# Block-sparse attention with a channel mix on one core: another order of the units, one finishing pass, and other numbers in the planner

## The chip, the cores and the metric

The kernel runs on one core of a Trainium2 chip. The core has four compute engines, each with its own instruction stream: TensorE (PE, matrix multiplies, with its weight loads shown as PEld), VectorE (DVE), ScalarE (ACT) and GpSimd (POOL). SyncE (SP) issues the DMA transfers here. The engines run side by side and wait for one another on semaphores. The metric is the device time of one execution in microseconds; less is better.

## The reference

The inputs are q, k and v (batch 4, 8 heads, 768 positions, 64 channels), a table of sampled blocks, two mixing vectors and three weight matrices. Positions are grouped into 24 blocks of 32. A block of queries looks at itself and its two neighbours, at the first and the last block, and at three sampled blocks; the first and the last block look at everything. On the attention's output stands a channel mix:

```python
scores = np.where(mask, scale * np.matmul(q, k.transpose(0, 1, 3, 2)), -1000000000.0)
attn = np.exp(scores - np.max(scores, axis=-1, keepdims=True))
attn = attn / (np.sum(attn, axis=-1, keepdims=True) + 1e-09)
x = np.matmul(attn, v)          # then laid out as (batch, 768, 512)
xk = mu_k * x + (1.0 - mu_k) * x_prev      # x_prev: one position back
xr = mu_r * x + (1.0 - mu_r) * x_prev
k = np.maximum(xk @ w_k, 0.0)              # 512 -> 1024
v = k * k @ w_v                            # 1024 -> 512
out = (1.0 / (1.0 + np.exp(-(xr @ w_r)))) * v
```

## The kernel before

**Units and tiles.** The attention is done in 26 units. A *wide* unit takes the first and the last block of one batch against all keys (4 of them, one for each batch); a *near* unit takes block n of all four batches against its eight blocks (22 of them, n = 1 to 22, called n1 to n22 below). The channel mix is done in 12 tiles of two blocks each: tile t takes blocks 2t and 2t+1 of all batches, and for the position before them the last row of block 2t−1. So tile 1 needs n1, n2 and n3, while tiles 0 and 11 need all four wide units.

**A near unit** loads q (scaled on POOL), keys into the buffer KA and values into VA; it computes scores (`s`, PE) in two halves of four heads, the row maximum (`nm`, DVE), the exponential (`p`, ACT), transposes (`t` on PE, copied to `pt` by ACT or DVE), the product with the values (`o`, PE), the division by the row sum (`R`, `x`, DVE), and a last transpose (`tx`, PE) that ACT copies into the tile `xt`. A wide unit does the same with names that carry a w: `sw`, `nmw`, `pw`, `tw`, `ptw`. KA and VA are one buffer each, which wide and near units share: a wide unit takes half of KA, and near units hold the last three blocks in a ring of slots and the sampled blocks in slots of their own.

**A tile of the mix** is split into a high and a low part (`xr`, `xk`: POOL, DVE, ACT and POOL in turn), then come on PE two gates (`r`, 12 multiplies each), four hidden groups (`h`, 24 each) and two value sums (`v`, 24 each), since every product is made of three.

**Weights.** The 20 pieces of w_r, w_k and w_v arrive as 64-bit numbers of 512 KB each. Each is turned into 32 bits by one ACT pass and three DVE passes (L379, L383, L387) and split into a high and a low part (L397 or L399, and L401). The first twelve go through eight buffers `early_w`.

**The order of the work** is planned: each step is handed to a planner with an engine, a cost in ns, the buffers that it reads and writes, and a due time. The planner places the steps one at a time, by due time among those that can start soon, with its own costs of hops between engines, of transfers and of the matmul clock. Each engine's instruction stream, SP's queue of transfers among them, is the result, and each engine works strictly in that order. The due times are the tables at the end of the file (`UNIT_AT`, `MIX_AT`, `RAW_AT`, `WEIGHT_AT` and the offsets). In this kernel the four wide units come first:

```python
return [[(b, 0), (b, NB - 1)] for b in range(B)] + [[(b, n) for b in range(B)] for n in range(1, NB - 1)]
```

and the tiles of the mix run from 0 to 11. The accumulator of a near unit is two buffers of one bank, `o[0]` and `o[1]`, for four heads each, and `finish` divides each by itself.

## Time and profile before

| | |
|---|---|
| runs | 573.17, 574.13, 574.96 us; median 574.13 |
| the profiled execution | 573.36 us |
| its span, from the first to the last instruction | 571.5 us |
| busy: PE, PEld, DVE, ACT, POOL | 538.0, 441.8, 262.3, 295.2, 317.1 us |
| mean granted TensorE clock | 0.987 of full speed |
| moved by DMA | 86.08 MB, 151 GB/s over the span |
| chain that ended last | PE 75%, DMA 9%, POOL 7%, DVE 4% |

The span is read in stretches: in each, the engine (or the DMA) that is busy nearly all the time sets the pace there. In the order of time one sees a start of some 100 us in which transfers are close to their limit and PE sits idle for parts, and then a long stretch in which PE is busy throughout. The timeline of one engine tells when its groups of instructions began and what ended the idle time in front of them; the chain of waits tells which work ended last.

### The profile page before, as it was taken

To read this page: it belongs to the slowest core of one execution; us is meant where nothing else is said; L and a number is where in the kernel's file an instruction comes from. 1 tells how busy PE (TensorE), PEld (TensorE's weight loads), DVE (VectorE), ACT (ScalarE), POOL (GpSimd) and SP (SyncE) were. 2 spreads that over 40 slices of the span, in tenths; PEclk is the share of its full clock that TensorE was granted. 3 is DMA by queue.
4 is the path that set the end of the run, shared out by engine and by line. 5 is a ranking of instruction groups with operands and counts; after the bars stand their busy time and mean duration, and the time that the engine had idled before them with its cause. 6 is when DMAs were issued, how large, how long until landed. Compare 5 with 4: busy or idle time off the path is not lost.

```text
span 571.5 us, 18262 instructions
## 1 busy us (share of the span) xinstructions
PE 538.0 (94%) x7724; PEld 441.8 (77%) x7724; DVE 262.3 (46%) x481; ACT 295.2 (52%) x594; POOL 317.1 (55%) x377
## 2 busy tenths in 40 slices
PE   8678768999999999999999999999999999999997
PEld 3445545777797897897897887897798898989896
DVE  1677998864434324337325345415434424242401
ACT  2536477675656445467456456556555543424241
POOL 1322657897465384475275456466167265677670
PEclk8979998999999999999999999999999999999999
DMA  8999899734442624454543272445323000000001
GB/s 319 367 387 367 303 315 346 267 120 147 133 148 78 220 77 129 154 169 132 194 142 114 93 225 89 146 160 188 117 89 95 21 21 19 18 21 18 33 5 38
DMA packets 34181, 86.08 MB, mean 151 GB/s; under 512 B 5010, under 2 KB 5780, under 8 KB 31124
## 3 DMA queue, kind: packets, MB, share of 16 engines
q1 hardware_dynamic: 34100, 84.92, 44.2%
q8 instruction: 61, 1.00, 0.7%
q14 instruction: 20, 0.16, 0.1%
HBM read 78.60 MB, written 6.29 MB: 149 GB/s over the span
## 4 chain that ended last, share of the span: by engine, by line
PE 75%; DMA 9%; POOL 7%; DVE 4%; SPq 3%; issue 2%; ACT 1%; POOLq 0%; ACTq 0%
PE v L821 23%; PE o L586 7%; PE s L562 6%; PE t L526 6%; PE r_0p L774 5%; PE h_0p L792 5%; PE r_1p L774 5%; PE h_3p L792 5%; PE h_2p L792 5%; PE h_1p L792 5%; DMA q<-qt 3%; DMA VA<-vw 2%; DMA KA<-kt 2%; POOL q L464 2%; PE tx L666 2%
## 5 line engine op out<-in xcount | busy, mean ns | idle before, releaser
L821 PE MATMUL v<-wv,k 128*128 128x512 f32 (+1 forms) x600 | 144.8, 391 | 1.1 <-POOL wv L401 1.1
L821 PEld LDWEIGHTS v<-wv,k 128*128 128x128 f32 x600 | 106.6, 188 | 24.5 <-POOL wv L401 1.5
L542 ACT ACTIVATE p<-s,nm 128x256 f32<-128x256 f32 x176 | 71.7, 484 | 20.6 <-DVE nm L570 20.5
L464 POOL TENSOR_SCALAR q<-q 128x512 f32<-128x512 f32 (+1 forms) x26 | 36.6, 1409 | 45.8 <-DMA q<-qt 25.1
L570 DVE TENSOR_REDUCE nm<-s 128x4 f32<-128x1024 f32 x44 | 52.8, 1217 | 13.5 <-PE s L562 13.1
L530 ACT COPY pt<-t 128x512 f32<-128x512 f32 x68 | 39.6, 587 | 37.4 <-PE t L526 34.8
L526 PE MATMUL t<-ident,p 128*128 128x128 f32 x352 | 54.5, 278 | 3.8 <-ACT pt L530 2.1
L586 PEld LDWEIGHTS o<-VA,pt 128*32 128x32 f32 x2816 | 42.2, 109 | 13.3 <-issue 10.4
L586 PE MATMUL o<-VA,pt 128*32 128x65 f32 x2816 | 49.5, 222 | 2.9 <-ACT pt L530 1.9
L526 PEld LDWEIGHTS t<-ident,p 128*128 128x128 f32 x352 | 40.6, 141 | 14.8 <-ACT pt L530 2.9
L562 PE MATMUL s<-KA,q 64*32 64x256 f32 x1408 | 44.9, 383 | 4.0 <-DMA KA<-kt 1.7
L750 POOL TENSOR_TENSOR xr<-xr_1f,xr 128x256 fp32r<-128x256 f32 x24 | 17.9, 744 | 38.5 <-ACT xr L748 38.5
L829 DVE SCALAR_TENSOR_TENSOR z<-v,z 128x512 f32<-128x512 f32 (+1 forms) x25 | 16.7, 669 | 48.4 <-PE v L821 48.4
L741 DVE SCALAR_TENSOR_TENSOR xr_1f<-xr_1d,mk,xt 128x128 f32<-128x128 f32 x48 | 17.1, 355 | 47.5 <-POOL xr L750 39.7
L738 POOL TENSOR_TENSOR xr_1d<-xt 128x128 f32<-128x128 f32 x48 | 20.5, 427 | 31.8 <-DVE xr_1f L741 24.0
L792 PE MATMUL h_1p<-xk,wk 128*128 128x256 f32 x288 | 36.9, 282 | 0.0
L562 PEld LDWEIGHTS s<-KA,q 64*32 64x32 f32 x1408 | 25.2, 106 | 15.1 <-issue 2.4
L792 PE MATMUL h_0p<-xk,wk 128*128 128x256 f32 x288 | 36.8, 282 | 0.0
L774 PE MATMUL r_0p<-wr,xr 128*128 128x512 f32 x144 | 36.7, 400 | 0.0
L792 PE MATMUL h_3p<-xk,wk 128*128 128x256 f32 x288 | 36.5, 281 | 0.0
L792 PE MATMUL h_2p<-xk,wk 128*128 128x256 f32 x288 | 36.1, 281 | 0.0
L738 POOL TENSOR_TENSOR xr_0d<-xt 128x128 f32<-128x128 f32 x48 | 19.4, 403 | 30.1 <-DVE xr_0f L741 20.7
(138 smaller groups left out, 962.4 us busy)
## 6 DMA issues: line engine op xcount, KB each, us to landing
VA<-vt SPq DMA_DIRECT2D x93, 260.0 KB, 3.8
KA<-kt SPq DMA_DIRECT2D x90, 256.0 KB, 3.7
VA<-vw SPq DMA_DIRECT2D x24, 260.0 KB, 6.5
KA<-kq SPq DMA_DIRECT2D x16, 384.0 KB, 6.4
out<-z SPq DMA_DIRECT2D x23, 256.0 KB, 2.0
q<-qt SPq DMA_DIRECT2D x22, 256.0 KB, 4.3
early_w<-w_k SPq DMA_DIRECT2D x8, 512.0 KB, 7.3
raw<-w_v SPq DMA_DIRECT2D x8, 512.0 KB, 6.1
```

The lines of the kernel that those rows point to most:

```text
L464: plan.add(POOL, 90 + 0.95 * HP * many * BLK, due, lambda: nc.gpsimd.tensor_scalar(out=q.ap[:, 0 : HP * many * BLK], in0=q.ap[:, 0 : HP * ...
L526: nc.tensor.transpose(tp.ap[:, i, :], p.ap[:, x : x + P], ident.ap)
L530: plan.add(ACT, 200 + 0.75 * P * many, rank + 0.1, lambda: nc.scalar.copy(pt.ap[:, 0:many], tp.ap[:, 0:many]), reads=[(tp,)], writes=[(pt,)])
L542: plan.add(ACT, 262 + 0.83 * width, rank, lambda: nc.scalar.activation(p.ap[:, out], view(), AF.Exp, bias=nm()), reads=[(s,), key[0]], wri ...
L562: nc.tensor.matmul(s.ap[ROWS[j], row, a * 256 : (a + 1) * 256].rearrange("p (c x t) -> p c t x", c=2, t=QB), q.ap[half, (hp * QB + j) * BL ...
L570: nc.vector.tensor_reduce(out=nm.ap.rearrange("p (r a) -> p r a", r=2), in_=s.ap.rearrange("p r (a x) -> p r a x", a=2), axis=AX.X, op=ALU ...
L586: nc.tensor.matmul(o[gi].ap[ROWS[j], i * DV : (i + 1) * DV], pts[row].ap[:, 2 * a + g, ROWS[j]], VA.ap[:, c0 + g, j, h * DV : (h + 1) * DV ...
L738: sub.tensor_tensor(out=parts(d.ap), in0=cols(c, 0), in1=cols(c, 1), op=ALU.subtract)
L750: plan.add(POOL, 80 + 2.4 * MIX * tw, rank + O_MIX, lambda f=f, cs=cs: nc.gpsimd.tensor_tensor(out=dst.ap[:, 1, cs], in0=f.ap, in1=dst.ap[ ...
L774: nc.tensor.matmul(pr.ap[:, 0:512], xr.ap[:, a, c, :], wr.ap[:, w, c, :], start=(c == 0 and m == 0), stop=(c == CC - 1 and m == 2))
L792: nc.tensor.matmul(ph.ap[:, ff * TT : (ff + 1) * TT], wk.ap[:, w, c, f * P : (f + 1) * P], xk.ap[:, a, c, :], start=(c == 0 and m == 0), s ...
L821: nc.tensor.matmul(pv.ap[:, 0:width], k2.ap[:, a, f, i * P : (i + 1) * P], wv.ap[:, w, f, cs], start=(f == 0 and m == 0), stop=(f == FC - ...
```

## The change

The change has four parts. The first two say what is computed when; the third changes the numbers and rules with which the order is planned; the fourth moves some work between engines or buffers.

1. One wide unit comes first, then the 22 near units, then the three other wide units. The tiles run in the order 1 to 10, 0, 11.
2. A near unit's accumulator is one buffer of two banks. `finish` makes one sum pass, one reciprocal and one product over all eight heads, where it made two of each. From unit 5 on the scores of both halves are one step for the planner.
3. The planner counts a slowdown of DVE beside POOL, has other costs (q's scaling on POOL, the weight passes, the mix), counts large transfers at a smaller size, and all due times are new.
4. The high part of the last eight weights is made by POOL and not by ACT (`HI_POOL` is 20 instead of 12); `pt` has four buffers instead of three; DVE's turn at a transposed copy (`TURN_FROM`, a count of units) begins at n6 instead of n3; the last two tiles use the accumulator banks in another rotation.

```diff
-    return [[(b, 0), (b, NB - 1)] for b in range(B)] + [[(b, n) for b in range(B)] for n in range(1, NB - 1)]
+    wide = [[(b, 0), (b, NB - 1)] for b in range(B)]
+    return wide[:1] + [[(b, n) for b in range(B)] for n in range(1, NB - 1)] + wide[1:]
...
+    def beside(self, at, ns, slow):
+
+        end = at + ns
+        for _ in range(4):
+            end = at + ns + slow * sum(max(0.0, min(end, b) - max(at, a)) for a, b in self.pool[-6:])
+        return end
...
-                     writes=[(raw,)], release=at, size=524288)
+                     writes=[(raw,)], release=at, size=455000)
...
-            plan.add(DVE, 480, rank, shift, reads=[(mag,)], writes=[(mag,)])
-            plan.add(DVE, 800, rank, sign, reads=[(mag,), (raw,)], writes=[(mag,)])
-            plan.add(DVE, 800, rank, tail, reads=[(mag,), (raw,)], writes=[(f,)])
+            plan.add(DVE, 430, rank, shift, reads=[(mag,)], writes=[(mag,)], slow=0.53)
+            plan.add(DVE, 690, rank, sign, reads=[(mag,), (raw,)], writes=[(mag,)], slow=0.35)
+            plan.add(DVE, 690, rank, tail, reads=[(mag,), (raw,)], writes=[(f,)], slow=0.35)
...
-        plan.add(POOL, 90 + 0.95 * HP * many * BLK, due, lambda: nc.gpsimd.tensor_scalar(
+        plan.add(POOL, 90 + 2.45 * HP * many * BLK, due, lambda: nc.gpsimd.tensor_scalar(
...
+        if once:
+            plan.add(PE, 2 * N_S, t0, lambda: [mm() for mm in both_mm], reads=scores_of, writes=[(s,) for s in both_s], table="scores", code=128)
...
-        for i in range(len(o)):
-            each = slice(4 * i, 4 * i + 4)
...
+        own = o.ap[:, 0:many, 0 : 4 * DV].rearrange("p i (h d) -> p i h d", d=DV)
+        r = R.ap[:, 0 : 4 * many].rearrange("p (i h) d -> p i h d", i=many)
+
+        def recip():
+            nc.vector.tensor_scalar(out=r, in0=own[:, :, :, D:DV], scalar1=1e-9, scalar2=None, op0=ALU.add)
+            nc.vector.reciprocal(r, r)
+
+        plan.add(DVE, 345 + 10 * many, rank, recip, reads=[(o, *parts)], writes=[(R,)])
+        plan.add(DVE, 70 + 352 * many, rank, lambda: nc.vector.tensor_tensor(
+            out=x.ap[:, 0 : many * 256].rearrange("p (i h d) -> p i h d", i=many, d=D), in0=own[:, :, :, 0:D],
+            in1=r.to_broadcast([P, many, 4, D]), op=ALU.mult), reads=[(o, *parts), (R,)], writes=[(x,)])
...
-            o = [buf([P, 4 * DV], F32, "o", 2, f"o{i}_{k}", ps) for k in range(1 if wide_one else 2)]
+            o = buf([P, 2, 512], F32, "o", 1, f"o{i}", ps)
...
-            tags = [("m", M_BUFS), ("o", 2), ("s", 2), ("s", 2)]
+            tags = [("m", M_BUFS), ("s", 2), ("m", M_BUFS), ("o", 1), ("s", 2)]
...
-        for t in range(NTILE):
-            last = t >= LAST
-            begin, rate = MIX_AT[t], MIX_RATE_LAST if last else MIX_RATE
+        for u, t in enumerate(TILES):
+            last = u >= LAST
+            begin, rate = MIX_AT[u], MIX_RATE_LAST if last else MIX_RATE
...
-XT_BUFS, P_BUFS, PT_BUFS, M_BUFS = 3, 4, 3, 2
+XT_BUFS, P_BUFS, PT_BUFS, M_BUFS = 3, 4, 4, 2
+ONCE_FROM, ONCE_PV_FROM, SECOND_ONCE = 5, 99, 3.0
...
-HI_POOL = frozenset(range(12))
+HI_POOL = frozenset(range(20))
...
+TILES = [*range(1, 11), 0, 11]
...
-UNIT_AT = [-16.20, -848.50, -2.86, -289.98, -1.90, 41.58, 72.35, 92.42, 104.53, 118.44, 133.49, 149.91, 161.10, 179.15, 191.08, 200.75, 208.39, 227.17, 242.81, 261.50, 276.37, 284.71, 307.53, 313.63, 386.56, 398.02]
...
```

What the planner makes of this is seen in each engine's order. PE's stream around the first gate, in the kernel before (`r_0p` is the gate of tile 0; `o_0_1435` and `o_1_1487` are the accumulators of n2, `o_0_1646` that of n3, `s_0_1546` and `s_1_1590` the scores of n4):

```order
155 L586 MATMUL o_0_1435<-VA,pt_0_1_1401 32x65 x16
156 L526 MATMUL t_0_0_1471<-ident,p_0_1413 128x128 x4
157 L586 MATMUL o_1_1487<-VA,pt_1_0_1405 32x65 x16
158 L586 MATMUL o_1_1487<-VA,pt_1_1_1479 32x65 x16
159 L526 MATMUL t_0_1_1528<-ident,p_0_1413 128x128 x4
160 L562 MATMUL s_0_1546<-KA,q_1210 32x2x4x32 x16
161 L666 MATMUL tx_1574<-ident,x_1524 128x128 x4
162 L526 MATMUL t_1_0_1580<-ident,p_1_1566 128x128 x4
163 L562 MATMUL s_1_1590<-KA,q_1210 32x2x4x32 x16
164 L526 MATMUL t_1_1_1614<-ident,p_1_1566 128x128 x4
165 L774 MATMUL r_0p<-wr,xr_0_1371 128x512 x6
166 L586 MATMUL o_0_1646<-VA,pt_0_0_1520 32x65 x16
```

and in the changed kernel (`r_0p` is the gate of tile 1, `o_83` the accumulator of n5, `s_0_1335` and `s_1_1352` the scores of n6, `s_0_1523` those of n7):

```order
112 L578 MATMUL s_0_1335<-KA,q_1010 32x2x4x32 x16
113 L578 MATMUL s_1_1352<-KA,q_1010 32x2x4x32 x16
114 L700 MATMUL tx_1380<-ident,x_1331 128x128 x4
115 L544 MATMUL t_1_0_1387<-ident,p_1_1312 128x128 x4
116 L614 MATMUL o_83<-VA,pt_0_0_1372 32x65 x16
117 L614 MATMUL o_83<-VA,pt_0_1_1377 32x65 x16
118 L544 MATMUL t_1_1_1435<-ident,p_1_1312 128x128 x4
119 L807 MATMUL r_0p<-wr,xr_0_1114 128x512 x12
120 L614 MATMUL o_83<-VA,pt_1_0_1431 32x65 x16
121 L614 MATMUL o_83<-VA,pt_1_1_1462 32x65 x16
122 L544 MATMUL t_0_0_1512<-ident,p_0_1440 128x128 x4
123 L578 MATMUL s_0_1523<-KA,q_1201 32x2x4x32 x16
```

Before, the first gate stands behind four wide units, the scores of n1 to n4 and all of n1 and n2; now it stands behind one wide unit, the scores of n1 to n6, all of n1 to n4 and half of n5's product.

SP's queue at the start of the program, before (`kq` and `vw` are a wide unit's keys and values, `w_r` and `w_k` weights):

```order
1 L470 DMA KA<-kq 128x768 x2
2 L462 DMA q_102<-qt 128x256
3 L470 DMA KA<-kq 128x768 x2
4 L474 DMA VA<-vw 128x520 x6
5 L365 DMA early_w<-w_r 128x1024
6 L365 DMA early_w<-w_k 128x1024 x3
7 L470 DMA KA<-kq 128x768 x2
8 L365 DMA early_w<-w_r 128x1024
9 L462 DMA q_136<-qt 128x256
```

and now (`q_167` belongs to n1, `q_169` to the wide unit, `kt` are keys of near units):

```order
1 L383 DMA early_w<-w_r 128x1024
2 L488 DMA KA<-kq 128x768 x2
3 L383 DMA early_w<-w_k 128x1024
4 L488 DMA KA<-kq 128x768 x2
5 L326 DMA number<-blocks 1x144
6 L327 DMA con<-seen 1x462
7 L383 DMA early_w<-w_k 128x1024
8 L383 DMA early_w<-w_r 128x1024 x2
9 L383 DMA early_w<-w_k 128x1024
10 L480 DMA q_167<-qt 128x512
11 L480 DMA q_169<-qt 128x256
12 L383 DMA early_w<-w_k 128x1024
```

Weights and the block table have moved to the front of the queue; the first wide unit's q, third before, now has six weights, its keys and n1's q ahead of it.

PE's stream in the changed kernel where the second wide unit's product begins (`v_0_0_6471` and `v_1_0_6589` belong to tile 8, `sw_0_0_6536` to the third wide unit, `o_119` is the second's accumulator):

```order
421 L854 MATMUL v_0_0_6471<-wv,k_6237 128x512 x9
422 L544 MATMUL tw_0_0_6493<-ident,pw_0_0_6097 128x128 x4
423 L854 MATMUL v_0_0_6471<-wv,k_6237 128x512 x12
424 L544 MATMUL tw_0_1_6524<-ident,pw_0_0_6097 128x128 x2
425 L544 MATMUL tw_0_1_6524<-ident,pw_0_1_6099 128x128 x2
426 L854 MATMUL v_0_0_6471<-wv,k_6237 128x512 x3
427 L641 MATMUL sw_0_0_6536<-KA,q_5876 64x384 x2
428 L641 MATMUL sw_0_1_6539<-KA,q_5876 64x384 x2
429 L641 MATMUL sw_0_0_6536<-KA,q_5876 64x384 x2
430 L641 MATMUL sw_0_1_6539<-KA,q_5876 64x384 x2
431 L544 MATMUL tw_0_2_6550<-ident,pw_0_1_6099 128x128 x4
432 L671 MATMUL o_119<-VA,ptw_0_0_6514 32x65 x16
```

Before, the eighth tile's sums (tile 7) stood among near units:

```order
456 L821 MATMUL v_0_0_6811<-wv,k_6585 128x512 x18
457 L666 MATMUL tx_6843<-ident,x_6804 128x128 x4
458 L821 MATMUL v_0_0_6811<-wv,k_6585 128x512 x6
459 L821 MATMUL v_1_0_6861<-wv,k_6585 128x512 x24
460 L526 MATMUL t_0_0_6906<-ident,p_0_6504 128x128 x4
461 L562 MATMUL s_0_6912<-KA,q_6430 32x2x4x32 x16
```

Three wide units, which stood at the start of the program, now stand between the matmuls of tiles 8 to 10.

## Rows read from the trace of the kernel before

**Rows 1.** Busy time in five stretches of the span: for each engine the busy us and, in brackets, the number of instructions, then the granted TensorE clock, the DMA engines' busy share and GB/s.

```profile
0.00:60.00 60.00, 46.33 (x805) 26.64 (x808) 35.48 (x68) 27.05 (x43) 16.48 (x24) 0.91 0.96 353
60.00:101.00 41.00, 29.48 (x785) 19.83 (x779) 38.52 (x60) 27.01 (x62) 26.20 (x29) 0.96 0.92 325
101.00:137.00 36.00, 32.52 (x488) 26.87 (x488) 25.88 (x42) 24.21 (x50) 32.32 (x31) 1.00 0.60 201
137.00:472.00 335.00, 333.53 (x5049) 283.48 (x5050) 135.77 (x268) 185.51 (x381) 183.46 (x222) 1.00 0.40 126
472.00:571.50 99.50, 96.16 (x620) 84.95 (x609) 26.71 (x45) 31.47 (x60) 58.69 (x75) 1.00 0.06 22
```

**Rows 2.** PE's timeline in the start: start us, length us, line, what, count, and in brackets the idle time in front and what ended it. The rows are the scores of n1, of n4 (two halves), the first gate, and the four waits after it.

```profile
67.84 1.10 PE L562 MATMUL s<-KA,q 64*32 64x256 f32 x32 [1.70 <-DMA KA<-kt]
...
95.86 1.71 PE L562 MATMUL s<-KA,q 64*32 64x256 f32 x32
...
99.79 1.09 PE L562 MATMUL s<-KA,q 64*32 64x256 f32 x32
...
101.23 1.65 PE L774 MATMUL r_0p<-wr,xr 128*128 128x512 f32 x6
...
111.02 0.66 PE L526 MATMUL t<-ident,p 128*128 128x128 f32 x4 [0.16 <-ACT h_0k L805]
...
114.84 0.66 PE L526 MATMUL t<-ident,p 128*128 128x128 f32 x4 [1.79 <-ACT pt L530]
...
125.11 0.66 PE L526 MATMUL t<-ident,p 128*128 128x128 f32 x4 [0.43 <-ACT h_3k L805]
...
136.57 2.83 PE L821 MATMUL v<-wv,k 128*128 128x512 f32 x11 [1.10 <-POOL wv L401]
```

**Rows 3.** The chain of waits in order of time: start us, length us, what. A DMA row's length runs from its issue to its landing.

```profile
54.02 1.45 PE sw L607 x16
...
61.03 6.68 DMA KA<-kt
...
88.08 3.14 DMA VA<-vt
...
445.54 1.89 PE s L562 x64
...
451.69 1.05 PE o L586 x64
...
540.20 2.80 PE r_0p L774 x12
543.00 2.83 PE h_0p L792 x24
...
554.31 2.80 PE r_1p L774 x12
557.11 11.06 PE v L821 x72
```

**Rows 4.** The page's list of DMA issues: what, engine, operation, count, KB each, median us from issue to landing.

```profile
VA<-vt SPq DMA_DIRECT2D x93, 260.0 KB, 3.8
KA<-kt SPq DMA_DIRECT2D x90, 256.0 KB, 3.7
VA<-vw SPq DMA_DIRECT2D x24, 260.0 KB, 6.5
KA<-kq SPq DMA_DIRECT2D x16, 384.0 KB, 6.4
...
q<-qt SPq DMA_DIRECT2D x22, 256.0 KB, 4.3
early_w<-w_k SPq DMA_DIRECT2D x8, 512.0 KB, 7.3
```

**Rows 5.** PE's timeline in the dense stretch: start us, length us (the ends are modelled, so the next start tells what a group cost).

```profile
447.36 0.66 PE L526 MATMUL t<-ident,p 128*128 128x128 f32 x4
447.77 1.65 PE L774 MATMUL r_0p<-wr,xr 128*128 128x512 f32 x6
...
451.10 0.60 PE L526 MATMUL t<-ident,p 128*128 128x128 f32 x4
451.62 1.12 PE L586 MATMUL o<-VA,pt 128*32 128x65 f32 x64
```

**Rows 6.** Groups of DVE instructions from 0 to 60 us: line, operation, shapes, count, busy us, mean ns, and idle time in front with its releaser.

```profile
L387 DVE SCALAR_TENSOR_TENSOR wf<-early_w,wmag 128x512 int32<-128x512 int32 x7 | 6.3, 901 | 0.0
L383 DVE SCALAR_TENSOR_TENSOR wmag<-early_w,wmag 128x512 int32<-128x512 int32 x7 | 5.0, 718 | 0.1
L379 DVE TENSOR_SCALAR wmag<-wmag 128x512 int32<-128x512 int32 x8 | 4.6, 599 | 2.2 <-ACT wmag L374 2.2
```

**Rows 7.** The same from 60 to 135 us.

```profile
L570 DVE TENSOR_REDUCE nm<-s 128x4 f32<-128x1024 f32 x10 | 12.1, 1215 | 2.7 <-PE s L562 2.7
L379 DVE TENSOR_SCALAR wmag<-wmag 128x512 int32<-128x512 int32 x12 | 10.0, 850 | 1.1 <-ACT wmag L374 1.1
L383 DVE SCALAR_TENSOR_TENSOR wmag<-raw,wmag 128x512 int32<-128x512 int32 x8 | 9.3, 1160 | 0.1
L387 DVE SCALAR_TENSOR_TENSOR wf<-raw,wmag 128x512 int32<-128x512 int32 x8 | 6.5, 806 | 1.6 <-POOL wv L401 1.5
```

116 lines of the change are left out of this document (66 added, 50 removed).

## The prediction, made before the changed kernel ran

> **What bounds the kernel now.** I read the stretches of the span first [rows 1]. From 137 to 472 us PE is busy 333.5 of 335 us, while no other engine passes 186 and the DMA is busy 40% of the time: there PE alone sets the pace. From 472 us on PE works off the last tiles. In front of it lies another kernel: from 0 to 60 us DMA is busy 96% of the time at 353 GB/s and PE idles 13.7 us; from 60 to 101 us DMA is at 92%, DVE at 38.5 of 41 us, and PE idles 11.5 us. So the start is bound by transfers first and then by transfers and DVE together, and the rest by PE. Next I read PE's timeline for the border between the two [rows 2]: the first gate of a tile starts at 101.23 us. After it PE loses 0.16, 1.79, 0.43 and 1.10 us in listed waits, 3.5 us in all. Last comes the chain of waits [rows 3]: its end is PE, 557.11 + 11.06 = 568.2 us, and 3.3 us more to the end of the span for the last product and store.
>
> The amount of matmul work doesn't change, so the time is: the moment of the first gate, plus PE work that is still to do then, plus what PE loses afterwards, plus 3.3 us. The change moves the first two against each other.
>
> **PE work, in prices of the dense stretch.** A tile costs two gates of 2.80, four hidden groups of 2.83 and 11.2 for its value sums (rows from 540 to 568 us) [rows 3], together 28.1, and by the distance of the starts 28.0. Scores of a near unit cost 1.89, a half of its products 1.05, a wide half's scores 1.45 [rows 3]. Four transposes cost 0.41 before a gate and 0.52 before products by the distance of starts [rows 5]; I take 0.5. A near unit is then 1.89 + 2×1.05 + 4×0.5 + 0.5 = 6.5, a wide one 2×1.45 + 6×0.5 + 192/64×1.05 + 0.3 = 9.3. In all 12×28.0 + 22×6.5 + 4×9.3 = 516 us.
>
> In front of the first gate stood four wide units (37.2), scores of n1 to n4 (7.6), twelve transposes (6.0), products of n1 and n2 (4.2) and two `tx` (1.0): 56 us. So 460 were left at 101.2, and 568.2 − 101.2 − 460 = 7 us were lost after it: the 3.5 us of waits and 3.5 that no row names. Now there stand one wide unit (9.3), scores of n1 to n6 (11.3), twenty transposes (10.0), products of four and a half units (9.5) and four `tx` (2.0): 42 us. So 474 are left. The first gate must come 14 us earlier, at 87.2 us, for nothing to change at all.
>
> **When the first gate comes.** It stands behind the scores of n6, and those behind n6's last keys. In the new queue there are up to these keys 15 weights, 4 and 6 loads of the wide unit, 29 key blocks, 24 value blocks, 7 q of near units and one of half that size; with the sizes of [rows 4] that is 7.9 + 1.6 + 1.6 + 7.6 + 6.4 + 2.0 = 27.0 MB. The rate is from before: keys issued at 61.03 landed at 67.7 behind 22.9 MB, values issued at 88.08 landed at 91.2 behind 31.4 MB [rows 3], so landing is about 1 us + MB/0.346. That gives 79.0 us. Before, n4's keys stood behind 31.9 MB, which gives 93.2, and its scores began at 95.86 [rows 2], a lag of 2.7; n1's had none. I take 2.2: 81.2 us. Then come on PE 1.89 (scores), 0.5 (`tx`), 0.5, 1.05, 0.5 = 4.4. Before, the stretch from n4's scores to the gate took 5.4 us for 3.4 of work [rows 2], so 2 us of waits; I take half, since both score halves now stand together and one finishing pass feeds `tx`. First gate: 86.6 us, between 82 (no lag, no wait, faster transfers: 353 GB/s as in the first minute of work [rows 1]) and 92 (below).
>
> SP's own order: six weights and n1's q now stand in front of the first wide unit's q, 5.1 MB, so it starts at about 17 us where it began at 7. That delays n1's ring keys, which wait until the wide scores have been read, but these stand behind 11.5 MB anyway (34 us). PE idles longer in front of it, and the granted clock, 0.91 on average before in the first 60 us [rows 1], may be lower there; at half clock the wide unit's 9.3 us double, inside 17 us in which PE waits for transfers, so I count nothing, and 3 us if n1 waits for it.
>
> **The other edits.** One finishing pass for eight heads saves DVE one sum and one reciprocal in 22 units; it bears on the path only in the start, and there it is in the half of the waits that I dropped. Its price is that the next unit's products wait for the whole accumulator; in the new order at least a `tx`, which waits for the same product, or 6 us of other matmuls stand between, so nothing. Eight high parts go from ACT to POOL, which was busy 32.3 of 36 us from 101 to 137 [rows 1]. There the last w_v piece ended PE's wait of 1.10 us; I bound the new wait by 0 and 3 and take 1. The ACT copies cost 2.4 us in three listed waits; with a fourth `pt` buffer I take 1. With the 3.5 unnamed that is 5.5 us lost after the gate, where 7 were. Merged scores change no matmul. The last two tiles work from other banks, with no wait listed there before: nothing.
>
> **Sum.** 86.6 + 474 + 5.5 + 3.3 = 569.4 us of span, 2.1 less than 571.5. The profiled execution was 573.36 us, 1.9 over its span, so 571.3 us. That execution is 0.8 below the median of 574.13, so I do not lean on a part of a microsecond: about 0.5% faster than the median.
>
> **The rivals.**
>
> *Nothing is gained.* The gate comes at 87 to 89 us. The bytes in front of it fell by a fifth, but PE work in front of it fell by a quarter, and both were made of the same units: earlier start, longer rest. 572 to 575 us. It takes only 2 us more lag than I chose.
>
> *DVE becomes the pace of the start (slower).* Each weight takes three DVE passes: 0.60 + 0.72 + 0.90 = 2.2 us up to 60 us [rows 6], but 0.85 + 1.16 + 0.81 = 2.8 us later, when POOL is busy [rows 1, 7]. POOL will now be busy from 20 us on with q's, weights and high parts. Up to n5's maxima DVE has 13 weights (28.9 at the low price), five units' maxima (10×1.215 [rows 7]) and some 17 us of table work, wide maxima, copies, products and mixing: 58 us from about 9 us on, against 77 us by the keys. So 10 us are free, of which unavoidable waits for scores take about 7. At the high price 13×0.6 = 7.8 us more are wanted and some 2.5 are there: the gate comes 5.3 us later, at 92, and the time is 576.6. It decides from the point where DVE has no idle time left between the maxima of n2 and n5. Against it: in the old start the dear passes were dear beside mixing and weights of the same kind, and DVE kept up with n4 within 2.7 us. [...]
>
> *The late wide units hold PE up (slower).* Their keys and values can load only when near units have released KA and VA. In the first 60 us, mostly wide units, PE idled 13.7 us [rows 1], 3.4 for each; three of them late would give 10, and 579 us. Against it: the DMA is at 6% there [rows 1], and between n22's last product and the first late wide product stand some 12 us of gate, value sums and transposes, against 6.5 us of landing [rows 4].
>
> *Much is gained.* The gate comes at 82 and only the unnamed 3.5 us are lost: 82 + 474 + 3.5 + 3.3 = 562.8, a time of 564.7. It needs transfers at 353 GB/s throughout and DVE never late.
>
> **How the numbers follow.** My forecast has a chance of 0.50, with a range of its own of 568 to 575 us; nothing gained 0.10; DVE 0.20; late wide units 0.08; much gained 0.12. A measurement of this kernel can tell about 0.3%, 1.7 us, from no change. The forecast gives faster 0.31, same 0.15, slower 0.04; nothing gained gives same 0.08 and 0.01 on each side; DVE gives slower 0.17, same 0.03; the wide units slower 0.07, same 0.01; much gained faster 0.12. Together faster 0.44, same 0.27, slower 0.29. The range reaches to the much gained below and past DVE's above: 563.5 to 580.
>
> **What would show it.** The first gate in PE's timeline: at 86 to 87 us I am right, at 82 the last rival, past 90 the second. The scores of n6 at 81 us show the rate. DVE's idle time in front of the maxima from 40 to 80 us: near nothing speaks for the DVE rival, and the mean of L383 near 1.1 us. From the gate on PE should lose about 5.5 us, none of it before the late `sw` and `o` rows; waits there of more than 2 us for transfers show the third. I would be wrong altogether if the dense stretch had other prices than before.

## The result, and the profile after

| | before | changed |
|---|---|---|
| median of ten runs each, side by side, us | 573.65 (571.88 to 574.96) | 576.58 (575.65 to 581.22) |
| ratio, 95% interval | 1 | 1.0068 (1.0046 to 1.0089) |
| span of the profiled execution, us | 571.5 | 576.8 |

The change made the kernel slower by 0.7%. The forecast was 0.5% faster; the time lies inside the range, on the other side of the kernel before. The profiled execution of the changed kernel lies 2.1 us above its median and that of the kernel before 0.3 below its own, so of the 5.3 us between the two traces some 2.4 belong to these two executions.

The stretches of the changed kernel, with the columns of [rows 1]:

```profile
0.00:60.00 60.00, 34.61 (x618) 20.99 (x626) 36.97 (x68) 24.83 (x48) 28.51 (x30) 0.77 0.93 338
60.00:101.00 41.00, 34.42 (x900) 26.47 (x883) 30.62 (x50) 27.92 (x66) 31.68 (x34) 0.96 0.86 283
101.00:137.00 36.00, 32.50 (x475) 27.48 (x474) 23.93 (x31) 21.01 (x42) 30.90 (x32) 0.95 0.59 196
137.00:472.00 335.00, 332.43 (x4964) 281.62 (x4963) 132.85 (x219) 184.26 (x367) 179.61 (x217) 1.00 0.42 134
```

The DMA engines are busy 93% and 86% of the first two stretches, where they were busy 96% and 92% [rows 1]: transfers do not run at the old rate. DVE is busy 30.6 us of 41 from 60 to 101 us, where it was 38.5. From 101 to 137 us PE idles 3.5 us, as before.

PE's timeline of the changed kernel: the first wide unit, scores of n1, products of n1 and n3, scores of n6 (the first 43 of 64), the first gate, and every wait above 0.5 us behind it.

```profile
21.61 2.84 PE L641 MATMUL sw<-KA,q 64*64 64x384 f32 x16 [15.02 <-POOL q L482]
...
37.78 3.50 PE L578 MATMUL s<-KA,q 64*32 64x256 f32 x64 [1.88 <-DMA KA<-kt]
...
51.97 3.27 PE L614 MATMUL o<-VA,pt 128*32 128x65 f32 x128 [3.02 <-DMA VA<-vt]
...
71.53 3.75 PE L614 MATMUL o<-VA,pt 128*32 128x65 f32 x128 [2.27 <-DMA VA<-vt]
...
85.15 1.52 PE L578 MATMUL s<-KA,q 64*32 64x256 f32 x43
...
90.77 3.02 PE L807 MATMUL r_0p<-wr,xr 128*128 128x512 f32 x12
...
116.64 2.92 PE L807 MATMUL r_1p<-wr,xr 128*128 128x512 f32 x6 [3.49 <-ACT h_3k L838]
...
194.52 0.31 PE L614 MATMUL o<-VA,pt 128*32 128x65 f32 x6 [1.10 <-issue]
...
318.64 1.57 PE L825 MATMUL h_1p<-xk,wk 128*128 128x256 f32 x11 [1.47 <-issue]
```

The first gate came at 90.77 us, 3.6 later than the 87.2 at which nothing changes, and behind it stands one new wait of 3.49 us that ends with ACT's `h_3k`. In sums: from the first gate to the end of the span there were 470.3 us, of which PE was busy 462.0 and idle 8.3; now there are 486.0, busy 476.65 and idle 9.4 (PE's busy time summed over stretches of 100 us from the gate on). So the gate gave 10.5 us, the longer rest took 14.7, and 1.1 more were lost: 5.3 us.

The queue of SP in the first 95 us tells how loads were held for PE's scores and products: line and what it waited for, us in all, times, longest. The two largest such waits, first of the changed kernel, then of the kernel before:

```profile
SPq L480 <- PE s L578: 8.7, 5, 4.2
SPq L471 <- PE o L614: 7.0, 4, 3.7
```

```profile
SPq L474 <- PE o L637: 3.2, 2, 3.0
SPq L444 <- PE s L562: 2.9, 1, 2.9
```

In the changed kernel a unit's q waits for the scores that still read its place, a value load for products; before, it was values of a wide unit and a key load. These waits grew from 6.1 to 15.7 us. That the near units now fill the queue from 31 us on and no longer from 61 would explain it; no run shows it.

### The profile page after: what moved, and what is told of

The parts are those of the page before. It is cut to its first block, busy times and chain, and to the rows that moved or that the text cites. A ratio compares the mean times of both kernels' runs of the same rounds, so it can differ in the third digit from the quotient of the medians.

```text
span 576.8 us, 18182 instructions
## 1 busy us (share of the span) xinstructions
PE 535.5 (93%) x7724; PEld 446.7 (77%) x7724; DVE 250.1 (43%) x412; ACT 291.4 (51%) x587; POOL 329.1 (57%) x385
## 4 chain that ended last, share of the span: by engine, by line
PE 82%; DMA 7%; POOL 5%; DVE 2%; issue 1%; SPq 1%; ACT 1%; POOLq 0%; DVEq 0%
PE v L854 23%; PE s L578 6%; PE r_1p L807 6%; PE o L614 6%; PE h_3p L825 6%; PE t L544 6%; PE h_1p L825 6%; PE h_0p L825 6%; PE r_0p L807 5%; PE h_2p L825 5%; DMA q<-qt 3%; PE sw L641 2%; PE tw L544 2%; DMA KA<-kt 2%; PE tx L700 2%; POOL q L482 2%
## 5 line engine op out<-in xcount | busy, mean ns | idle before, releaser
L482 POOL TENSOR_SCALAR q<-q 128x512 f32<-128x512 f32 (+1 forms) x26 | 40.1, 1542 | 36.2 <-DMA q<-qt 31.6
L548 ACT COPY pt<-t 128x512 f32<-128x512 f32 x71 | 41.1, 591 | 35.0 <-PE t L544 32.3
L614 PEld LDWEIGHTS o<-VA,pt 128*32 128x32 f32 x2816 | 44.6, 114 | 14.9 <-issue 11.9
L544 PE MATMUL t<-ident,p 128*128 128x128 f32 x352 | 53.0, 277 | 0.5 <-ACT p L560 0.4
L807 PE MATMUL r_1p<-wr,xr 128*128 128x512 f32 x144 | 37.5, 409 | 3.5 <-ACT h_3k L838 3.5
L825 PE MATMUL h_0p<-xk,wk 128*128 128x256 f32 x288 | 38.0, 285 | 0.0
L825 PE MATMUL h_3p<-xk,wk 128*128 128x256 f32 x288 | 37.9, 285 | 0.0
L774 DVE SCALAR_TENSOR_TENSOR xr_0f<-xr_0d,mk,xt 128x128 f32<-128x128 f32 x48 | 21.0, 438 | 37.4 <-POOL xk L783 15.6
L825 PEld LDWEIGHTS h_0p<-xk,wk 128*128 128x128 f32 x288 | 36.1, 189 | 1.3 <-issue 0.4
```

The source lines that it names most:

```text
L482: plan.add(POOL, 90 + 2.45 * HP * many * BLK, due, lambda: nc.gpsimd.tensor_scalar(out=q.ap[:, 0 : HP * many * BLK], in0=q.ap[:, 0 : HP * ...
L544: nc.tensor.transpose(tp.ap[:, i, :], p.ap[:, x : x + P], ident.ap)
L548: plan.add(ACT, 200 + 0.75 * P * many, rank + 0.1, lambda: nc.scalar.copy(pt.ap[:, 0:many], tp.ap[:, 0:many]), reads=[(tp,)], writes=[(pt,)])
L614: nc.tensor.matmul(o.ap[ROWS[j], gi, i * DV : (i + 1) * DV], pts[row].ap[:, 2 * a + g, ROWS[j]], VA.ap[:, c0 + g, j, h * DV : (h + 1) * DV ...
L774: nc.vector.scalar_tensor_tensor(out=parts(f.ap[:, i, :]), in0=parts(d.ap), scalar=mk.ap[:, which, c : c + 1], in1=cols(c, 1), op0=ALU.mul ...
L807: nc.tensor.matmul(pr.ap[:, 0:512], xr.ap[:, a, c, :], wr.ap[:, w, c, :], start=(c == 0 and m == 0), stop=(c == CC - 1 and m == 2))
```

## The experiments

The theories: A, the queue of loads is held because places for keys, values and q come free late; bytes, the forecast's own step, that the amount in the queue alone sets when data land; B, PE at half its clock (granted at 0.50 from 21.6 to 25.0 us of the changed kernel) makes the start late; C, the late first wide unit does; D, POOL's added copies cost the time behind the gate.

A kernel has the changed kernel's plan (before_hi_pool that of the kernel before); the edits act on its finished list: `move(a, b)` puts operation a directly ahead of b, with a third argument 1 directly behind it. "Gate" is the start of the first gate in the profiled execution, "idle" is PE's idle time from there to the end of the span. Two profiled executions of one kernel (`hi_warm`, `hi_warm_again`) differ by 0.6 us in the gate and 1.3 in the idle time, and hi_act and hi_two_pass, which are equally fast, by 1.4 in the gate; so a difference of 1 or 2 us in these columns carries nothing. The five kernels with one execution add loads, or leave out loads or passes, to see what these are worth; their time stands in place of a ratio.

| kernel | ratio to before (95%) | gate | idle |
|---|---|---|---|
| before | 1 | 101.23 | 8.3 |
| changed | 1.0068 (1.0046 to 1.0089) | 90.77 | 9.4 |
| hi_act | 0.9996 (0.9976 to 1.0016) | 89.39 | 6.5 |
| before_hi_pool | 1.0098 (1.0073 to 1.0123) | 104.38 | 8.2 |
| hi_two_pass | 0.9997 (0.9978 to 1.0016) | 90.78 | 5.7 |
| wide_first | 1.0056 (1.0030 to 1.0082) | 89.77 | 9.5 |
| values_first | 1.0098 (1.0071 to 1.0125) | 90.08 | 9.2 |
| ring_act | 1.0148 (1.0115 to 1.0180) | 95.38 | 8.6 |
| hi_values_soon | 1.0029 (1.0002 to 1.0055) | 88.60 | 7.5 |
| hi_values_soon2 | 1.0047 (1.0026 to 1.0067) | 91.36 | 6.5 |
| hi_extra | one execution, 575.35 us | 92.60 | 5.8 |
| hi_less | one execution, 570.89 us | 88.76 | 4.8 |
| hi_thin_dve | one execution, 571.74 us | 88.85 | 6.0 |
| hi_light | one execution, 567.83 us | 85.02 | 5.6 |
| hi_light_thin | one execution, 562.28 us | 80.33 | 5.1 |
| hi_warm | 0.9958 (0.9931 to 0.9985) | 88.25 | 3.5 |
| hi_warm_again | 0.9978 (0.9958 to 0.9999) | 87.67 | 4.8 |
| hi_warm_on | 0.9986 (0.9962 to 1.0009) | 93.11 | 3.7 |
| hi_short_warm | 1.0004 (0.9981 to 1.0026) | 90.81 | 3.9 |
| warm | 1.0059 (1.0032 to 1.0086) | 92.30 | 6.9 |

### POOL's eight high parts

hi_act, in `weight`:

```diff
-            plan.add(POOL, 650, rank, lambda: nc.gpsimd.tensor_copy(dst()[:, 0, :], f.ap), reads=[(f,)], writes=[(owner, (0, key))])
+            by = nc.gpsimd.tensor_copy if i < 12 else nc.scalar.copy
+            plan.add(POOL, 650, rank, lambda: by(dst()[:, 0, :], f.ap), reads=[(f,)], writes=[(owner, (0, key))])
```

> The changed kernel with its plan kept; the eight high parts of w_v are copied by ACT again, as in the kernel before, and not by POOL. Theory D (POOL's added copies make h_1k's pass and so r_1p late): POOL has 8 x 0.65 us less to do between 90 and 125 us, the wait of 3.5 us ahead of r_1p falls below 1.5, the time falls by 2 to 3 us to about 574. Theory A, B and C: the gate stays at 90 to 91; the wait stays at 3 or more because POOL's pass over h_1k stands behind a scaling of q that waits for its transfer; time 576 to 577.

Measured: level with the kernel before, and 0.7% below the changed kernel. POOL and then ACT of the changed kernel in front of the new wait:

```profile
103.46 1.72 POOL L482 TENSOR_SCALAR q<-q 128x512 f32<-128x512 f32 x1 [1.33 <-DMA q<-qt]
...
114.70 1.26 POOL L842 TENSOR_TENSOR k<-h_1k,k 128x512 fp32r<-128x512 f32 x1
```

```profile
115.99 0.60 ACT L838 ACTIVATE h_3k<-h_3p 128x512 f32<-128x512 f32 x1 [3.94 <-POOL k L842]
```

ACT's pass over the fourth hidden group needs one of three `kk` buffers, and POOL frees it with the low part of the second group, at 114.70 + 1.26 = 116.0 us; `r_1p` waits for ACT. Its first six products then take 2.92 us: from 116.2 to 119.4 us the granted clock was 0.50, and 1.00 from there to 137. One of the eight copies stands just ahead of POOL's wait for q, one between it and that low part. PE's timeline with the copies on ACT, with the scores of n6:

```profile
84.21 2.75 PE L579 MATMUL s<-KA,q 64*32 64x256 f32 x64
...
89.39 3.03 PE L808 MATMUL r_0p<-wr,xr 128*128 128x512 f32 x12
...
111.64 1.67 PE L808 MATMUL r_1p<-wr,xr 128*128 128x512 f32 x6
...
188.13 0.31 PE L615 MATMUL o<-VA,pt 128*32 128x65 f32 x6 [0.55 <-issue]
...
312.22 1.47 PE L826 MATMUL h_1p<-xk,wk 128*128 128x256 f32 x11 [1.53 <-issue]
```

`r_1p` has no wait, and its first six products take 1.67 us. Behind the gate PE idles 2.9 us less than in the changed kernel and is busy 475.53 us where it was busy 476.65: 4.0 us in all, about as much as the ratios say. `r_1p` has no wait in any kernel below whose name begins with `hi_`, and 2.9 to 3.5 us in all that have the changed order and the copies on POOL (3.43 in wide_first, 2.92 in values_first, 2.97 in ring_act, 3.29 in warm). POOL still waits 1.16 us for the same q in hi_act, so the q doesn't decide. But the copies act in two ways that these runs don't part. POOL's low part of the second group comes at 112.00 us in hi_act, 2.7 sooner, of which 1.4 are the earlier gate; and the fourth group gets another of the three buffers there, one that DVE and not POOL frees, as ACT's row in hi_act shows:

```profile
110.99 0.60 ACT L839 ACTIVATE h_3k<-h_3p 128x512 f32<-128x512 f32 x1 [0.52 <-DVE wf L405]
```

The same part alone, put into the kernel before:

```diff
-            plan.add(ACT, 520, rank, lambda: nc.scalar.copy(dst()[:, 0, :], f.ap), reads=[(f,)], writes=[(owner, (0, key))])
+            by = nc.gpsimd.tensor_copy if i >= 12 else nc.scalar.copy
+            plan.add(ACT, 520, rank, lambda: by(dst()[:, 0, :], f.ap), reads=[(f,)], writes=[(owner, (0, key))])
```

> The kernel before, with only this part of the change: the eight high parts of w_v are copied by POOL and not by ACT, at the same places of the order. Theory D (the price of the change is POOL's added copies): slower by 2 to 4 us, 575 to 577. If D holds only together with the late q of the changed start, or the gain of the run with the copies on ACT came from something else: within 1 us of the kernel before.

Measured: 1.0098, 5.6 us, more than any theory had. Its PE timeline, first gate and first products with w_v:

```profile
104.38 1.87 PE L775 MATMUL r_0p<-wr,xr 128*128 128x512 f32 x6
...
140.18 0.49 PE L822 MATMUL v<-wv,k 128*128 128x512 f32 x1 [0.61 <-POOL wv L400]
...
141.56 4.37 PE L822 MATMUL v<-wv,k 128*128 128x512 f32 x11 [0.89 <-POOL wv L402]
```

The gate is 3.2 us later than in [rows 2], and eleven products that took 2.83 us there took 4.37, from 141.56 to 145.93 us: the granted clock was 0.95 from 124.4 to 144.4 us and 0.96 from there to 164.4, where it was 1.00 before from 121.2 to 161.2. By these means some 3.6 us stood at 0.50, an estimate. `r_1p` has no wait here. Behind the gate PE idles as long as before, 8.2 us, but is busy 465.75 us where it was busy 461.98. So the copies cost time in both orders, and not at the same place. Why the gate is later no run shows.

### The joint finish

`sums` and `heads` are the sum with its reciprocal, and the product, of four heads.

```diff
-        plan.add(DVE, 345 + 10 * many, rank, recip, reads=[(o, *parts)], writes=[(R,)])
...
+        plan.add(DVE, 345 + 10 * many, rank, lambda: sums(0), reads=[(o, *parts)], writes=[(R,)])
+        plan.add(DVE, 70 + 352 * many, rank, lambda: [heads(0), sums(1), heads(1)], reads=[(o, *parts), (R,)], writes=[(x,)])
```

> The changed kernel with the eight high parts of w_v back on ACT, and each near unit finished in two sets of passes of four heads each, as in the kernel before (six instructions on DVE in place of three). If the joint finish is worth nothing on the path: 572.5 to 573.5, as with the high parts on ACT alone. If it hides part of the late start: 574 to 576, 0.1 us for each of 22 near units or more. Faster than 572 is expected by no theory.

Measured: 0.9997 against 0.9996 with the joint finish, each within 0.2%: it is worth nothing that can be told here. What else came with the change (the fourth `pt` buffer, DVE's later turn at copies, the other rotation of banks, the planner's numbers) no run parts from the order.

### The order of the loads

wide_first:

```diff
+    for one in (named["q", 0], *[named["kq", 0, k] for k in range(4)]):
+        move(one, head)
+    move(named["scale", 0], named["scale", 1])
```

> The changed kernel with its plan kept; only the wide unit's q and its four key loads are put at the head of SP's queue, ahead of the weights, and POOL scales this q before unit n1's. The wide unit can then start at about 7 us instead of 21.6. Theory C (the late wide unit holds up all that follows it): the first gate comes 5 us or more earlier, at about 85, and the time falls by 4 to 5 us to about 572. Theory of bytes (the queue's bytes alone pace the start, as the prediction had it): n1's keys stand behind the same 12.5 MB, n1's scores stay at about 37, the gate at 90 to 91, the time at 576 to 577. Theory A (loads are held until places for keys and values come free, from n1 on): n1's scores stay at about 37, what follows gains 1 to 2 us because the wide unit's products are out of the way, gate about 89, time about 575.

```profile
7.22 0.83 PE L642 MATMUL sw<-KA,q 64*64 64x384 f32 x2 [0.64 <-DMA KA<-kq]
...
24.88 1.97 PE L545 MATMUL tw<-ident,pw 128*128 128x128 f32 x8 [14.95 <-ACT pw L657]
...
35.77 1.96 PE L579 MATMUL s<-KA,q 64*32 64x256 f32 x64 [0.74 <-issue]
...
89.77 3.03 PE L808 MATMUL r_0p<-wr,xr 128*128 128x512 f32 x12
```

PE's timeline shows that the wide unit began at 7.2 us, but its transposes stayed at 24.9, since ACT's exponentials wait for maxima that stand behind weights in DVE's order. n1's scores came 2.0 us earlier, the gate 1.0, the time is the same. So theory C was tested only in part; that the wide unit's first scores are late costs nothing that can be told.

values_first (`hoist` moves with an operation what it needs):

```diff
+    for row in range(2):
+        hoist(named["ow", 0, 0, row], named["s", 1, 1])
+    for one in first[0:4] + first[6:7]:
+        hoist(one, named["q", 3])
```

> The changed kernel with its plan kept; on PE the wide unit's last products stand ahead of n1's scores, and on SP the five value loads behind them stand ahead of the q, ring key and picked keys that wait for n1's scores. No byte is added or taken away. Theory A (held places): n1's values are issued at about 39 instead of 44.9, n1's products run at about 46 instead of 52.0, the gate comes 3 to 5 us earlier, the time falls to 572 to 574. Theory of bytes: gate and time as before, 90 to 91 and 576 to 577. Theory B (a PE at half its clock makes the start late) and theory C (late wide unit): no change either.

ring_act:

```diff
-            keys_from(RING + (n + 1) % 3, n + 1, at_k)
+            named["ring", i] = keys_from(RING + (n + 1) % 3, n + 1, at_k, by=nc.scalar if 2 <= n <= RING_ACT else nc.sync)
...
+    for n in range(2, RING_ACT + 1):
+        move(named["ring", n], max((named["exp", n - 1, gi, 0] for gi in range(2)), key=ops.index))
```

> The changed kernel with its plan kept; the one ring key load of each of the units n2 to n7 is issued by ACT ahead of the exponentials of the second half of the unit before, and no longer by SP. Theory A (SP's queue stands held at its head, and a ring key waits behind what SP issues): the units' scores come every 8.4 to 9 us instead of every 9.84, the gate 3 us earlier, the time about 573.5; against it stand six issues on ACT of some 0.4 us each. Theory of bytes: the same bytes in nearly the same order, gate 90 to 91, time 576 to 577. If what paces is the values and not the keys, also no change.

Neither gained. In values_first n2's scores waited 4.53 us for their q, which now stood behind the values, and n1's products came at 53.0 us, not 46; in ring_act the gate came 4.6 us later. In values_first, what is taken from one load's wait is paid by another's; so theory A in this form (SP's order is the trouble) got no support. With the copies on ACT it was tried once more, with loads that nobody waits for yet put back:

```diff
+    for n in range(2, 7):
+        move(named["picked", n + 1], named["pickedv", n], 1)
```

> The changed kernel with the eight high parts of w_v back on ACT; on SP, for n = 2 to 6, the three picked key loads of unit n+1 stand behind the value loads of unit n and no longer ahead of them (they are needed a unit later). The same bytes, the same places. Theory A, made sharper (units n1 to n6 run in a chain: products, SP's issue of the next values, their landing, the next products; the values are late because SP first issues keys that nobody waits for yet): the waits for transfers of values ahead of the products shrink, the first gate comes 2 to 4 us earlier than 89.4, the time falls to 569.5 to 571.5. Theory of bytes: gate and time as with the high parts on ACT alone, 89 to 91 and 572 to 574. If the picked keys come late instead: gate at 91 or later, time 574 or more.

and, in hi_values_soon2, with two loads of w_v put back as well:

```diff
+    for i, n in ((17, 4), (16, 5)):
+        move(raws[i], named["picked", n + 1], 1)
```

> As the run before, and two loads of w_v (0.52 MB each) that stood ahead of the values of n3 and of the picked ones of n5 are put behind the picked keys of those rounds. Theory A: a further 0 to 2 us at the gate, time 569 to 571. Theory of bytes: 572 to 574. If w_v then comes late for its passes: the waits ahead of the first products with w_v (about 117 us) grow, and the time is no better than 572.

Measured: 1.0029 and 1.0047, no gain. n1's products did begin 3.6 us sooner than in hi_act (47.5 us, 51.1 there), and n3's scores came at the same 56.0 us, after waits of 1.73 and 2.21 us that end with nothing the profile shows (`issue`, in hi_act 0.55 there). Whether these waits or the order kept the gain back is open.

### Bytes, DVE, or both

hi_extra and hi_less, bytes added and taken away:

```diff
+    extras = {id(named["q", n + 1]): 2 * (n - 3) for n in range(3, 7)}
...
+        k = extras.get(id(op))
+        if k is not None:
+            extra(k)
+            extra(k + 1)
```

> The changed kernel with the eight high parts of w_v back on ACT, and eight more loads of 0.26 MB on SP's queue, two ahead of each of the loads of q for n4 to n7, into a place that nothing reads. They hold nothing and wait for nothing; all eight stand ahead of n6's last keys. Theory of bytes: 2.1 MB at the 0.346 MB a us of the kernel before are 6.1 us, so n6's scores at about 90.3 in place of 84.2 and the first gate at about 95. Theory A (the queue stands idle while its head is held): the loads go into the idle time, n6's scores come at most 2 us later, the gate at 90 to 91.5.

```diff
-            for j in range(NRAND):
+            for j in range(1 if 3 <= n <= 6 else NRAND):
```

> The changed kernel with the eight high parts of w_v back on ACT; units n3 to n6 load one picked value block and leave out the other two (their places keep older values). Six of the eight loads left out, 1.6 MB, stand ahead of n6's last keys. Theory of bytes: 4.6 us at 0.346 MB a us, so n6's scores at about 79.6 in place of 84.2 and the gate at about 84.8. Theory A: what holds the queue's head (scores and products of the units before) is the same, n6's scores come at most 2 us earlier, the gate at 87.5 to 89.5.

PE's timelines, scores of n6 and first gate, of hi_extra and then of hi_less:

```profile
87.41 2.19 PE L580 MATMUL s<-KA,q 64*32 64x256 f32 x64
...
92.60 3.04 PE L809 MATMUL r_0p<-wr,xr 128*128 128x512 f32 x12
```

```profile
83.38 1.74 PE L579 MATMUL s<-KA,q 64*32 64x256 f32 x42
...
88.76 3.02 PE L808 MATMUL r_0p<-wr,xr 128*128 128x512 f32 x12
```

Six microseconds of bytes more made n6's scores 3.2 us later than hi_act's 84.21, more than theory A allowed and half of what the theory of bytes did; 4.6 us less made them 0.8 earlier. Bytes alone do not pace the start. Nor does DVE alone, as hi_thin_dve shows: in the shift and in the sign, with `THIN` 16:

```diff
-                m = mag.ap.bitcast(I32)
+                m = mag.ap[:, 0:THIN].bitcast(I32)
```

> The changed kernel with the eight high parts of w_v back on ACT; of DVE's three passes over each weight, the shift and the sign work on 16 of 512 columns (the rest keeps unshifted values). Loads, orders and all other passes stay. Some 12 us of DVE's work between 38 and 90 us go. Theory of DVE (its passes stand ahead of the maxima and of the finish that n1 to n6 wait for): the first gate at 84 to 87, time 567 to 570. Theory A (places, landings and PE's own order): the gate at 88 to 90, time 571 to 573.

```profile
83.30 2.60 PE L579 MATMUL s<-KA,q 64*32 64x256 f32 x64
...
88.85 3.02 PE L808 MATMUL r_0p<-wr,xr 128*128 128x512 f32 x12
```

The gate moved by 0.5 us, no more than noise. Then loads in larger measure, keys and values alike, and both together (hi_light_thin has the edit above as well):

```diff
-            for j in range(NRAND):
+            for j in range(0 if 3 <= n <= 6 else NRAND):
```

> The changed kernel with the eight high parts of w_v back on ACT; units n3 to n6 leave out all six picked loads each, keys and values (their places keep older blocks). 5.5 MB less stand ahead of n6's scores, 16 us at 0.346 MB a us, and SP issues 21 loads less. If loads in any form (bytes, places, SP's issue) pace the start: gate at 85 or earlier. If the chain through PE, DVE and ACT of each unit paces it by itself: gate at 87 to 89.

> As hi_light, and of DVE's three passes over each weight the shift and the sign work on 16 of 512 columns. If loads and DVE's passes stand in parallel, each nearly as late as the other: gate 3 us or more earlier than with either alone, at 84 or earlier. If the chain through a unit's steps in PE's order is what paces: gate at 86 to 89 again.

PE's timeline of hi_light, and then of hi_light_thin: scores of n2, n5 and n6, the first gate, and in hi_light n3's `tx`.

```profile
43.50 3.36 PE L579 MATMUL s<-KA,q 64*32 64x256 f32 x64 [2.99 <-DMA VA<-vt]
...
68.98 1.09 PE L701 MATMUL tx<-ident,x 128*128 128x128 f32 x4 [2.73 <-DVE x L695]
...
70.85 3.67 PE L579 MATMUL s<-KA,q 64*32 64x256 f32 x64
...
79.82 2.19 PE L579 MATMUL s<-KA,q 64*32 64x256 f32 x64
...
85.02 3.04 PE L808 MATMUL r_0p<-wr,xr 128*128 128x512 f32 x12
```

```profile
43.24 2.11 PE L579 MATMUL s<-KA,q 64*32 64x256 f32 x64 [2.49 <-DVE wmag L401]
...
67.83 1.96 PE L579 MATMUL s<-KA,q 64*32 64x256 f32 x64
...
75.13 2.47 PE L579 MATMUL s<-KA,q 64*32 64x256 f32 x64
...
80.33 3.03 PE L808 MATMUL r_0p<-wr,xr 128*128 128x512 f32 x12
```

With 16 us of loads gone the gate moved by 4.4 us, and with DVE's passes thinned as well by 9.1. In PE's order a `tx` that waits for DVE, 2.73 us in hi_light, holds up the next scores. By the gates alone the passes would be worth 0.5 us while the loads stand and 4.7 when these are gone, as if the two stood in parallel, each nearly as late as the other. But the two traces differ in something else too. Their stretches from 30 to 90 us, with the columns of [rows 1], hi_light first:

```profile
30.00:90.00 60.00, 51.03 (x1362) 36.94 (x1362) 50.60 (x73) 44.34 (x103) 42.11 (x40) 0.91 0.68 224
30.00:90.00 60.00, 50.56 (x1410) 37.69 (x1398) 45.48 (x80) 46.40 (x106) 40.45 (x43) 1.00 0.74 244
```

PE's granted clock was 0.91 in hi_light, as in hi_act, and 1.00 in hi_light_thin. The scores of n2 and n5 alone took 3.0 us longer in hi_light. So the 4.4 us, noise of 1 or 2 apart, are the loads', but how much of the further 4.7 is DVE's passes and how much the clock is not shown.

### PE's clock, or its program

In `warm`, 75 (hi_warm, warm) or 81 (hi_warm_on) matmuls in place of 20; in hi_short_warm the 55 added ones have 8 columns.

```diff
-            for i in range(times):
+            for i in range(75):
```

> The changed kernel with the eight high parts of w_v back on ACT, and 75 in place of 20 matmuls on constants ahead of the first wide unit, so that PE is at work until the unit's q is there. Theory B (PE at half its clock makes the start late): the wide unit's scores take 1.4 us and not 2.8, the unit is through 2 to 3 us earlier, the first gate 2 us or more earlier, time 570 to 571. Theory A: n1's keys land at 37 as before, the gate stays at 89 to 91, time 572 to 574.

> The changed kernel with the eight high parts of w_v back on ACT and 75 matmuls ahead of the first wide unit, but the 55 added ones of 8 columns and not of 512: PE's program is shifted by as many instructions, and PE stands idle before the wide unit as with 20. Theory B (the clock): the wide unit runs at half the clock again, no gain, 572 to 574. Theory of the shift (waits for nothing that the profile shows fall at other places of PE's program): the waits behind the gate are as few as with 75 full ones, 570 to 571.

> The changed kernel as it stands, with 75 in place of 20 matmuls of 512 columns ahead of the first wide unit. If these gain by themselves what they gained beside the copies on ACT: 2 to 3 us, 573.5 to 575. If that gain was a matter of where PE's program happened to wait: anything from 575 to 577.

> The changed kernel with the eight high parts of w_v back on ACT and 81 in place of 20 matmuls ahead of the first wide unit, up to about 21.4 us. Theory B (the clock): the wide unit's scores take 1.4 to 1.6 us, time 569.5 to 571, as with 75 or better. If 75 gained by chance: 572 to 574.

> The same kernel as hi_warm, timed a second time. Theory B (the clock, 2 us): a ratio of 0.994 to 0.998 to the kernel before again. If the first median was chance: 0.998 to 1.001, as the kernel with the copies on ACT alone.

PE's timelines of hi_warm and of hi_short_warm:

```profile
21.80 2.25 PE L642 MATMUL sw<-KA,q 64*64 64x384 f32 x16 [2.23 <-POOL q L483]
...
54.64 1.09 PE L545 MATMUL t<-ident,p 128*128 128x128 f32 x8 [2.23 <-issue]
...
88.25 3.02 PE L808 MATMUL r_0p<-wr,xr 128*128 128x512 f32 x12
```

```profile
56.48 1.97 PE L545 MATMUL t<-ident,p 128*128 128x128 f32 x8 [3.97 <-issue]
...
90.81 3.03 PE L808 MATMUL r_0p<-wr,xr 128*128 128x512 f32 x12
```

hi_warm is 0.2 to 0.4% faster than the kernel before in two sets of runs, the second of them just clear of noise; it is the only version that beat both kernels. Why is not settled. Against theory B: hi_warm_on keeps PE at work until its first `sw`, which then takes 1.52 us, and cannot be told from the kernel before; in the profiled execution of hi_warm_again the first `sw` took 2.84 us, as without the added matmuls; warm gained nothing that can be told. Two things are seen: in all kernels with 55 or 61 more matmuls the two `issue` waits behind the gate (0.55 and 1.53 us in hi_act) are gone, whatever the columns, and another stands in the start, which in hi_short_warm is longer, 3.97 us, than what is saved behind the gate.

## Why the prediction was wrong

**The structure held.** PE's work from the gate on was to be 460 and 474 us; PE was busy 462.0 and 476.65, a difference of 14.7 for the 14 forecast (hi_act: 475.53, 13.6). From n6's scores to the gate it was to take 5.4 us and took 5.6. The late wide units wait for no transfer: after 116.64 us no wait above 0.5 us ends with one.

**The step that failed first: "landing is about 1 us + MB/0.346", taken for n6's keys.** It gave 79.0 and, with the lag of 2.2, scores at 81.2; they came at 85.15, and so the gate at 90.77 instead of 86.6. Up to n1 the step was right: to these keys there are 12.5 MB, that is 37.1 us, and n1's scores began at 37.78. From n1 on it was not: by bytes (27.0 − 12.5)/0.346/5 = 8.4 us a unit, measured (85.15 − 37.78)/5 = 9.5. And the right number stood in [rows 2]: from n1 to n4 the kernel before took (95.86 − 67.84)/3 = 9.3 us a unit. I had read these rows for a lag. With them the gate would have been forecast at 37.1 + 5 × 9.3 + 5.4 = 89.0, the span at 89.0 + 474 + 5.5 + 3.3 = 571.8 and the time at 573.7: no change, which is what hi_act is. That the old pace carries over so closely is seen once and not explained.

**What the pace is made of** is shown only in part. Not bytes alone: 4.6 us of them less moved n6's scores by 0.8. Loads in bulk are worth 4.4 us of the gate, but hi_light takes away bytes, places and SP's issues at once; that places come free late is seen in SP's waits and isolated by no run. DVE's passes are worth nothing that can be told while the loads stand; what they are worth without them is mixed with PE's clock. And the clock itself was put at nothing from n1 on: the prediction weighed it for the wide unit only. In the changed kernel it was granted at 0.50 from 37.8 to 40.9, 51.4 to 54.4 and 71.9 to 74.9 us, and the three groups that fell there (scores of n1, products of n1 and n3: 3.50, 3.27 and 3.75 us) took 4.4 us more than the prices of 1.89 and twice 2.1. How much of that moved the gate no run isolates.

**The second step: the loss of 5.5 us after the gate.** Idle behind the gate, with the 3.3 us at the end, was to be 8.8 and was 9.4, and PE's busy time came 2.0 us above its price before and 2.7 after: together 486.0 us behind the gate where 474 + 8.8 = 482.8 were forecast. The sum hides that one term was mis-sized: "I bound the new wait by 0 and 3 and take 1" for POOL's eight copies. They cost 4.1 us in this kernel (1.0068 to 0.9996), and not at w_v's products, where I looked, but ahead of `r_1p`, where a `kk` buffer came free late: 2.9 us more idle time and 1.1 us more busy time, the first products at a clock of 0.50. In the kernel before they cost 5.6 us at other places. In the timed runs this step weighs more than the first: of the 5.3 us between the forecast of 571.3 and the median of 576.58 some 3 are the copies (4.1 for 1), and some 2 are left for the gate. That the whole loss is nevertheless near the forecast comes from the rest: without those copies the new order idles 6.5 us where the old one idles 8.3.

**The rivals.** The DVE rival named a gate of 92 and 576.6 us, and both nearly came. That the time agrees is luck: 4.1 us of it are POOL's copies behind the gate, which this rival does not have, and DVE's passes alone moved the gate by 0.5. Its sign, no idle time in front of the maxima, was not seen: 4.5 us, all of them from 40 to 80 us. DVE from 38 to 90 us of the changed kernel, by groups:

```profile
L598 DVE TENSOR_REDUCE nm<-s 128x4 f32<-128x1024 f32 x11 | 13.3, 1218 | 4.5 <-PE s L578 4.4
L397 DVE TENSOR_SCALAR wmag<-wmag 128x512 int32<-128x512 int32 x8 | 5.5, 696 | 0.1
L405 DVE SCALAR_TENSOR_TENSOR wf<-early_w,wmag 128x512 int32<-128x512 int32 x6 | 5.0, 836 | 0.2
L401 DVE SCALAR_TENSOR_TENSOR wmag<-early_w,wmag 128x512 int32<-128x512 int32 x5 | 4.3, 867 | 0.1
```

Three passes took 0.70 + 0.87 + 0.84 = 2.4 us, nearer to the low price of 2.2 [rows 6] than to the high one of 2.8; the sign's 1.1 us for the second did not come. That they grow dearer where POOL is busy was my reading of [rows 6] and [rows 7], and no run isolates it. With POOL busy 34.4 of these 52 us, the means of 0.87 (L401) and 0.84 (L405) beside 0.72 (L383) and 0.90 (L387) in [rows 6], where POOL was busy 16.5 of 60, show little of it. Nor did the rows before speak for it as plainly as I read them: from [rows 6] to [rows 7] the means of L379 and L383 rose, from 0.60 to 0.85 and from 0.72 to 1.16, and that of L387 fell from 0.90 to 0.81. "Nothing is gained" was the right rival for the order and the finish, at 0.10; it had no room for POOL's copies. Its argument was stronger than I put it: by its own counts, 31.9 MB to n4's keys and 27.0 to n6's, the bytes fell by a sixth, not a fifth. The 579 us of the late wide units are a span; as a time they are 569.4 + 10 + 1.9 = 581.3, past the end of the range.

**The wide unit** began at 21.6 us, not 17, because POOL's two scalings of q took 4.43 us; wide_first shows that this cost nothing that can be told, as the forecast had it for another reason.

## What to carry to other kernels

Read the pace of a start from the distance of equal units in the old trace before you work it out from the bytes of one resource: it holds waits that the next version may inherit (here 9.3 us a unit before, 9.5 after, 8.4 by bytes). Where taking away one suspect moves nothing, take away two together before you acquit either, and compare the granted clock of the traces before you credit the second. Price work given to an engine that "has room" at whatever stands behind it in that engine's order, here a pass that frees one of three buffers and ended a wait of 3.49 us, and not only at the consumer of that work.
